# GEGLU feed-forward on one core: x's second half on ScalarE's queue, and six first products ahead of any second

## The chip, the cores and the metric

The kernel runs on one core of one Trainium2 chip. A core has five engines, each with its own instruction stream: TensorE (PE in the profile; its weight loads are PEld), VectorE (DVE), ScalarE (ACT), GpSimd (POOL) and SyncE (SP). Transfers from the chip's main memory run on 16 DMA engines that all of them share. SyncE and ScalarE can put a transfer on a queue of their own (q1 is SyncE's, q10 ScalarE's). The metric is the time of one execution on the device, in microseconds. The kernel before took 277.13 us (median of three runs, 276.82 to 277.15).

## The reference

```python
B, S, D, F = 32, 32, 1024, 3584
def reference(x, w_gate, w_up, w_down):      # x: (B, S, D), all bfloat16
    return (gelu_tanh(x @ w_gate) * (x @ w_up)) @ w_down
```

There are 1024 rows of x, so three products of 1024 x 1024 x 3584 have to be done.

## The kernel before, in words

The kernel has two stages. Stage 1 computes g = gelu(x w_gate) * (x w_up), transposed, into the tile `gT` (28 blocks of 128 columns of F, each 128 x 1024). Stage 2 multiplies g by w_down. Both replace eight half-size products of a 2 x 2 block scheme by seven, with sums of blocks formed on VectorE and GpSimd. Only the start of stage 1 is touched by the change.

**Names.** `B11`, `B21` are the two D halves of the first 512 rows of x, transposed (tile `xt0`); `B12`, `B22` are the D halves of the last 512 rows (tile `xt1`). x lies row by row in memory, so these are loaded with a transposing transfer (`dma_start_transpose`). `WG[c]` holds 256 columns of w_gate, which is two blocks of 128. Its D half `0:KH` (KH = 4 slices of 128) feeds a block's first product, its half `KH:DT` the second. `WU[c]` holds 512 columns of w_up.

**Blocks.** `first_products(i)` (lines 199 to 207) sends four matmuls of B11 with the first half of block i into a PSUM tile A[i], and ScalarE then copies A[i] to `E1`. `second_products(i)` (209 to 214) adds four matmuls with B21 to the same A[i], and ScalarE puts the gelu of it into `GL`. The second product of a block may begin only when ScalarE has copied A[i]. `seed(i)` (218) copies E1 into a PSUM tile X[i], which later products are added to. T1 to T4 are four sums of B11, B12, B21, B22, made on VectorE (`t_sum`, 158 to 161, called at 269 to 272), and they feed the products that come behind (`y` at 286, `x` in `sixth_products`, `seventh_products`, `fourth_product`).

**Order.** `tc.manual_schedule()` means that each engine runs its instructions in the order in which the code writes them. At the start TensorE multiplies a tile of zeros NWARM = 11 times (line 139). SyncE issues, in this order: B11 (131), B21 (144), the second half of gate tile 1 (145), gate tiles 2 and 3 (146, 147), half of w_up tile 0 (148), gate tile 4 (149), xt1 (150), gate tile 5 (151), the rest of w_up tile 0 (152). ScalarE issues three loads: the first half of gate tile 0 at the start (132), the first half of gate tile 1 behind the third multiplication of zeros, and the second half of gate tile 0 behind the eleventh (143). The first ten blocks are then worked in the groups (0 to 3), (4, 5), (6, 7), (8, 9): the first products of a group, then its second products (274 to 280).

The names `A` and `y` live in four PSUM tiles of tag `q`, the zeros' results and `X` in four of tag `p`.

Of the kernel before, what the change touches and what calls it, by code (L numbers as in the profile page):

```python
# [12 lines left out]
def kernel(  # L13
# [18 lines left out]
    nc = tc.nc  # L32
    P = nc.NUM_PARTITIONS
# [4 lines left out]
    xf = x.flatten_outer_dims()  # L38
    of = out.flatten_outer_dims()
    N, D = xf.shape  # L40
    F = w_gate.shape[1]
    NB = 512
    DT = D // P
    KH = DT // 2
# [2 lines left out]
    DB = 512  # L47
    NDB = D // DB
    assert N == 2 * NB and DT % 2 == 0 and D % DB == 0 and FT % 4 == 0
    NWARM = 11  # L50
    LEAD = 10
    ALONE = (4, 7, 10, 13, 16, 19, 22, 25)
    KF = FT // 2
# [22 lines left out]
    B11, B21 = xt0[:, :KH, :], xt0[:, KH:, :]  # L76
# [6 lines left out]
    def load_gate(c, queue, lo=0, hi=DT):  # L83
        if c not in WG:
            WG[c] = gw.tile([P, DT, 2 * P], bf16, name="gw", tag="gw")
        queue.dma_start(
            out=WG[c][:, lo:hi, :], in_=wg_r[:, lo:hi, 2 * c * P : (2 * c + 2) * P]
        )

    def load_up(c, lo=0, hi=4):  # L90
        if c not in WU:
            WU[c] = uw.tile([P, DT, 4 * P], bf16, name="uw", tag="uw")
        nc.sync.dma_start(
            out=WU[c][:, :, lo * P : hi * P],
            in_=wu_r[:, :, (4 * c + lo) * P : (4 * c + hi) * P],
        )
# [4 lines left out]
    def a11(i):  # L101
        return block(WG, 2, i, 0)

    def a12(i):
        return block(WG, 2, i, 1)
# [4 lines left out]
    def a22(i):  # L110
        return block(WU, 4, i, 1)
# [12 lines left out]
    def psum_p(name):  # L124
        return psum.tile([P, NB], fp32, name=name, tag="p")

    def psum_q(name):
        return psum.tile([P, NB], fp32, name=name, tag="q")

    with tc.manual_schedule():  # L130
        nc.sync.dma_start_transpose(out=B11, in_=xf[0:NB, 0 : KH * P])  # L131
        load_gate(0, nc.scalar, 0, KH)
        zt = opool.tile([P, NB], bf16, name="zt", tag="o")
        nc.vector.memset(zt, 0.0)
        warm = [psum_p("warm") for _ in range(4)]
# [2 lines left out]

        for n in range(NWARM):
            nc.tensor.matmul(warm[n % 4], lhsT=zt[:, 0:P], rhs=zt, start=True, stop=True)  # L140
            if n in (2, NWARM - 1):
                nc.scalar.activation(table, warm[n % 4][:, 0:8], ACT.Copy)
                load_gate(int(n == 2), nc.scalar, *((0, KH) if n == 2 else (KH, DT)))
        nc.sync.dma_start_transpose(out=B21, in_=xf[0:NB, KH * P : D])
        load_gate(1, nc.sync, KH, DT)
        load_gate(2, nc.sync)
        load_gate(3, nc.sync)
        load_up(0, 0, 2)
        load_gate(4, nc.sync)
        nc.sync.dma_start_transpose(out=xt1, in_=xf[NB:N, :])  # L150
        load_gate(5, nc.sync)
# [6 lines left out]
        def t_sum(name, a, b, step=2):  # L158
            for k in range(0, KH, step):
                ks = slice(k, k + step)  # L160
                nc.vector.tensor_tensor(T[name][:, ks, :], a[:, ks, :], b[:, ks, :], ALU.subtract)
# [19 lines left out]
        def copy_a22(i):  # L181
            nc.scalar.activation(C22[i], a22(i), ACT.Copy)

        A, E1, GL = {}, {}, {}

        def pair_product(ps, lhs, rhs, first, cuts):
            for lo, hi in zip(cuts, cuts[1:]):
                for p, l in zip(ps, lhs):
                    for k in range(lo, hi):
                        nc.tensor.matmul(  # L190
                            p,
                            lhsT=l[:, k, :],
                            rhs=rhs[:, k, :],
                            start=(first and k == 0),
                            stop=(k == KH - 1),
                            skip_group_check=True,
                        )

        def first_products(*blocks, cuts=(0, KH)):
            for i in blocks:  # L200
                A[i] = psum_q("a")
            pair_product([A[i] for i in blocks], [a11(i) for i in blocks], B11, True, cuts)
            for i in blocks:
                if i % 2 == 0:
                    pool, tag = (xpool, "e1") if i == LEAD - 2 else (ring, "ring")
                    E1[i // 2] = pool.tile([P, 2, NB], fp32, name="e1", tag=tag)
                nc.scalar.activation(E1[i // 2][:, i % 2, :], A[i], ACT.Copy)  # L207

        def second_products(*blocks, cuts=(0, KH)):
            pair_product([A[i] for i in blocks], [a12(i) for i in blocks], B21, False, cuts)  # L210
            for i in blocks:
                if i % 2 == 0:
                    GL[i // 2] = half.tile([P, 2, NB], bf16, name="gl0", tag="half")
                nc.scalar.activation(GL[i // 2][:, i % 2, :], A[i], ACT.Gelu_apprx_tanh)  # L214
# [3 lines left out]
        def seed(i):  # L218
            X[i] = psum_p("x")
            nc.scalar.activation(X[i], E1[i // 2][:, i % 2, :], ACT.Copy)  # L220
# [3 lines left out]
        def ahead():  # L224
            nonlocal done
            if done < FT:
                first_products(done)
            second_products(done - 1)
            done += 1
# [40 lines left out]
        t_sum("T2", B22, T["T1"])  # L270
        t_sum("T3", B22, B12)
        t_sum("T4", B21, T["T2"])
        between = {4: lambda: seed(0), 6: lambda: seed(1), 8: lambda: copy_a22(0)}
        for blocks in ((0, 1, 2, 3), (4, 5), (6, 7), (8, 9)):
            for n in blocks:
                first_products(n)
            if blocks[0] in between:
                between[blocks[0]]()
            for n in blocks:
                second_products(n)  # L280
        for k in range(KH):
            nc.scalar.activation(T["B22"][:, k, :], B22[:, k, :], ACT.Copy)
        copy_a22(1)
        for i in range(2):
            Y[i] = psum_q("y")
        pair_product(
            [Y[0], Y[1]], [S1[0], S1[1]], T["T1"], True, range(KH + 1)
        )
        first_products(LEAD)
        sixth_products(0, 1)  # L290
        first_products(LEAD + 1)
# [88 lines left out]
        B21 = lambda j: V21[j]  # L380
# [149 lines left out]
```

## Time and profile before

| what | from | value |
|---|---|---|
| median of three runs | the times | 277.13 us |
| profiled execution, time on the device | the times | 276.81 us |
| its span in the trace | the page | 275.0 us |
| TensorE busy | the page, part 1 | 269.7 us, 98% of the span |
| DMA engines, bytes moved | the page, part 3 | 26.42 MB, 96 GB/s over the span |
| first matmul of block 0 starts | the timeline | 6.14 us |
| first matmul of a second product starts | the timeline | 10.57 us |
| first product with T1 starts | the timeline | 24.19 us |
| last matmul of stage 1 and 2 | the timeline | about 271.5 us |

The span is counted from the first instruction that the trace holds; the execution's own time has some 1.8 us more around it. A matmul's duration in the rows (about 380 ns) is that of one passing through a filled pipeline; from start to start it is 0.216 us for the 128 x 512 shape in bfloat16, as 48 of them from 10.57 to 20.92 us show. "Landing" is the time from the issue of a transfer to its completion as seen by who waits for it.

### The profile page before, as it was taken

How to read it: one execution, taken by the hardware profiler on the slowest of the kernel's cores; microseconds unless marked ns; L12 is line 12 of the kernel's file. 1: busy time of each engine (PE TensorE's matmuls, PEld its weight loads, DVE VectorE, ACT ScalarE, POOL GpSimd, SP SyncE). 2: the span in 40 equal slices, each digit the busy share in tenths (PEclk: the TensorE clock that was granted, in tenths of full speed). 3: DMA queues.
4: the chain of work that ended last, by engine and by line, in shares of the span. 5: the costliest groups of instructions: out<-in, count | busy, mean ns of one | idle time of the engine just before them, and what ended most of it. 6: DMA issues, size and time to landing. Idle time of an engine off the chain costs nothing.

```text
span 275.0 us, 3348 instructions
## 1 busy us (share of the span) xinstructions
PE 269.7 (98%) x1187; PEld 189.9 (69%) x1187; DVE 189.1 (69%) x227; ACT 138.1 (50%) x238; POOL 87.1 (32%) x81
## 2 busy tenths in 40 slices
PE   8999999999999999999999999999999999999994
PEld 2345677768777687776877768764447888888883
DVE  0059875766667666676666766759994999999900
ACT  2578655656656666566665666531100072860311
POOL 0000073854558545585455854600000000000000
PEclk9999999999999999999999999999999999999999
DMA  8999402062400024216260202359602000000321
GB/s 170 279 288 254 155 1 76 25 206 80 150 2 0 0 87 145 76 31 199 87 220 0 76 2 77 117 181 328 216 0 76 2 0 0 1 2 0 116 76 38
DMA packets 40960, 26.42 MB, mean 96 GB/s; under 512 B 9200, under 2 KB 40944, under 8 KB 40944
## 3 DMA queue, kind: packets, MB, share of 16 engines
q1 hardware_dynamic: 39216, 25.30, 31.6%
q10 hardware_dynamic: 1728, 0.92, 1.3%
q8 instruction: 9, 0.15, 0.2%
q14 instruction: 7, 0.06, 0.1%
HBM read 22.02 MB, written 2.10 MB: 88 GB/s over the span
## 4 chain that ended last, share of the span: by engine, by line
PE 95%; DMA 3%; SPq 1%; ACT 0%; issue 0%
PE x L190 19%; PE x L385 18%; PE y L115 18%; PE a L190 16%; PE x L115 9%; PE y L385 9%; PE z L385 4%; DMA xt<-in_x_dram 3%; PE y L190 1%; SPq L131 1%; ACT o_sb L497 0%
## 5 line engine op out<-in xcount | busy, mean ns | idle before, releaser
L190 PE MATMUL x<-T,s 128*128 128x512 f32 x224 | 63.4, 407 | 0.0
L190 PEld LDWEIGHTS x<-T,s 128*128 128x128 f32 x224 | 41.8, 188 | 10.7
L190 PE MATMUL a<-xt,gw 128*128 128x512 bf16 x192 | 45.0, 382 | 0.6 <-DMA xt<-in_x_dram 0.5
L253 DVE TENSOR_TENSOR u<-y,e 128x512 bf16<-128x512 f32 x28 | 19.3, 692 | 33.0 <-ACT e L251 32.2
L179 POOL TENSOR_TENSOR s<-gw,s 128x512 fp32r<-128x512 bf16 x22 | 26.0, 1180 | 48.4 <-PE y L115 47.7
L190 PEld LDWEIGHTS <-gw 128*128 128x128 bf16 x192 | 17.5, 98 | 24.7 <-issue 5.7
L175 DVE TENSOR_TENSOR s<-s,gw 128x512 fp32r<-128x512 f32 x24 | 34.5, 1437 | 0.0
L260 ACT ACTIVATE gl<-h 128x512 bf16<-128x512 bf16 x28 | 17.7, 631 | 28.1 <-DVE h L258 28.1
L240 DVE TENSOR_TENSOR gT<-gl,x 128x512 bf16<-128x512 bf16 x28 | 19.2, 687 | 17.6 <-PE x L115 17.6
L115 PE MATMUL x<-T,c 128*128 128x512 f32 x112 | 30.3, 393 | 0.0
L115 PE MATMUL y<-B,s 128*128 128x512 f32 x112 | 30.2, 391 | 0.0
L170 POOL TENSOR_TENSOR s<-uw 128x512 fp32r<-128x512 bf16 x25 | 29.1, 1162 | 0.0
L115 PE MATMUL y<-T,s 128*128 128x512 f32 x104 | 27.8, 389 | 0.0
L385 PE MATMUL x<-tc,sc 128*128 128x512 f32 x112 | 25.7, 389 | 0.0
L207 ACT ACTIVATE e<-a 128x512 f32<-128x512 f32 x28 | 16.7, 597 | 16.5 <-PE a L190 16.5
L251 ACT ACTIVATE e<-x 128x512 f32<-128x512 f32 x28 | 16.7, 599 | 16.1 <-PE x L190 16.1
L171 POOL TENSOR_TENSOR s<-gw,uw 128x512 fp32r<-128x512 bf16 x21 | 24.4, 1161 | 0.0
L115 PEld LDWEIGHTS y<-B,s 128*128 128x128 f32 x112 | 21.0, 188 | 4.7
L115 PEld LDWEIGHTS x<-T,c 128*128 128x128 f32 x112 | 20.9, 188 | 4.8 <-ACT e L251 0.5
L385 PEld LDWEIGHTS x<-tc,sc 128*128 128x128 f32 x112 | 21.0, 188 | 4.4
L115 PEld LDWEIGHTS y<-T,s 128*128 128x128 f32 x104 | 19.5, 188 | 4.1
L214 ACT ACTIVATE gl<-a 128x512 bf16<-128x512 f32 x28 | 16.7, 596 | 6.8 <-PE a L190 6.5
(57 smaller groups left out, 342.0 us busy)
## 6 DMA issues: line engine op xcount, KB each, us to landing
uw<-in_w_up_dram SPq DMA_DIRECT2D x6, 1024.0 KB, 6.4
gw<-in_w_gate_dram SPq DMA_DIRECT2D x10, 512.0 KB, 4.0
v<-in_w_down_dram SPq DMA_DIRECT2D x5, 512.0 KB, 3.4
v<-in_w_down_dram SPq DMA_DIRECT2D x4, 640.0 KB, 7.9
v<-in_w_down_dram SPq DMA_DIRECT2D x8, 256.0 KB, 4.4
out_dram<-o_sb SPq DMA_DIRECT2D x15, 128.0 KB, 1.7
uw<-in_w_up_dram SPq DMA_DIRECT2D x2, 512.0 KB, 6.7
gT<-in_w_gate_dram SPq DMA_DIRECT2D x2, 512.0 KB, 6.1
```

The source lines that it names most:

```text
L115: nc.tensor.matmul(ps, lhsT=lhs[:, k, :], rhs=rhs[:, k, :], start=(first and k == 0), stop=(k == KH - 1), skip_group_check=True,)
L170: engine.tensor_tensor(S1[i], a21(i), a22(i), ALU.add)
L171: engine.tensor_tensor(S3[i], a11(i), a21(i), ALU.subtract)
L175: nc.vector.tensor_tensor(S2[i], S1[i], a11(i), ALU.subtract)
L179: engine.tensor_tensor(S4[i], a12(i), S2[i], ALU.subtract)
L190: nc.tensor.matmul(p, lhsT=l[:, k, :], rhs=rhs[:, k, :], start=(first and k == 0), stop=(k == KH - 1), skip_group_check=True,)
L207: nc.scalar.activation(E1[i // 2][:, i % 2, :], A[i], ACT.Copy)
L214: nc.scalar.activation(GL[i // 2][:, i % 2, :], A[i], ACT.Gelu_apprx_tanh)
L240: nc.vector.tensor_tensor(gT[:, i, 0:NB], GL[i // 2][:, i % 2, :], X[i], ALU.mult)
L253: nc.vector.tensor_tensor(U1[i], Y[i], e3, ALU.add)
L260: nc.scalar.activation(G1[i], h1, ACT.Gelu_apprx_tanh)
L385: nc.tensor.matmul(ps, lhsT=lhs[:, i, t * P : (t + 1) * P], rhs=rhs[:, i, :], start=(first and j == 0 and i == 0), stop=(last and j == JF ...
```

## The change

Three things are edited, all within the first 25 us.

1. **Loads.** B21 goes from SyncE's queue (second there) to ScalarE's, behind the third multiplication of zeros. ScalarE keeps one other load, a quarter of gate tile 0 (two of its eight slices). Everything else that ScalarE loaded is now on SyncE's queue, directly behind B11: the next quarter of gate tile 0, the first halves of gate tiles 1 and 2, the second half of tile 0, the second halves of tiles 1 and 2, the first half of tile 3, half of w_up tile 0 (so this lies between the halves of gate tile 3), the second half of gate tile 3, gate tile 4, and from there as before. In the built program, ScalarE's transpose waits for the completion of the transpose of B11, and SyncE's load of gate tile 4 waits for the completion of the transpose of B21.
2. **Order of products.** The first products of blocks 0 to 5 all come before any second product. Blocks 0 and 1 share their first products in two cuts: slices 0 and 1 of both blocks, then slices 2 and 3. A[4] and A[5] take PSUM tiles of tag `p`. `seed(0)` moves from behind block 5's first product to behind block 4's second product.
3. **Zeros.** NWARM is 10 in place of 11, and the second small activation on the zeros' result is gone.

The number of matmuls on x and the weights, the bytes loaded, the sums and the evictions are the same.

```diff
-    NWARM = 11
+    NWARM = 10
...
         nc.sync.dma_start_transpose(out=B11, in_=xf[0:NB, 0 : KH * P])
-        load_gate(0, nc.scalar, 0, KH)
+        load_gate(0, nc.scalar, 0, 2)
...
         for n in range(NWARM):
             nc.tensor.matmul(warm[n % 4], lhsT=zt[:, 0:P], rhs=zt, start=True, stop=True)
-            if n in (2, NWARM - 1):
+            if n == 2:
                 nc.scalar.activation(table, warm[n % 4][:, 0:8], ACT.Copy)
-                load_gate(int(n == 2), nc.scalar, *((0, KH) if n == 2 else (KH, DT)))
-        nc.sync.dma_start_transpose(out=B21, in_=xf[0:NB, KH * P : D])
+                nc.scalar.dma_start_transpose(out=B21, in_=xf[0:NB, KH * P : D])
+        for piece in ((0, 2, KH), (1, 0, KH), (2, 0, KH), (0, KH, DT)):
+            load_gate(piece[0], nc.sync, *piece[1:])
         load_gate(1, nc.sync, KH, DT)
-        load_gate(2, nc.sync)
-        load_gate(3, nc.sync)
+        load_gate(2, nc.sync, KH, DT)
+        load_gate(3, nc.sync, 0, KH)
         load_up(0, 0, 2)
+        load_gate(3, nc.sync, KH, DT)
         load_gate(4, nc.sync)
...
             for i in blocks:
-                A[i] = psum_q("a")
+                A[i] = psum_p("a") if i in (4, 5) else psum_q("a")
...
-        between = {4: lambda: seed(0), 6: lambda: seed(1), 8: lambda: copy_a22(0)}
-        for blocks in ((0, 1, 2, 3), (4, 5), (6, 7), (8, 9)):
-            for n in blocks:
-                first_products(n)
-            if blocks[0] in between:
-                between[blocks[0]]()
-            for n in blocks:
-                second_products(n)
+        between = {6: lambda: seed(1), 8: lambda: copy_a22(0)}
+        first_products(0, 1, cuts=(0, 2, KH))
+        for n in range(2, 6):
+            first_products(n)
+        for n in range(6):
+            second_products(n)
+            if n == 4:
+                seed(0)
+        for n in (6, 8):
+            first_products(n)
+            first_products(n + 1)
+            between[n]()
+            second_products(n)
+            second_products(n + 1)
```

## The prediction

> **What bounds the kernel now.** I read the page first, then the chain that ended last in its first 48 us, then the timeline of the first 25 us, then the DMA queues in stretches of 0.2 to 1 us.
>
> ```profile
> PE 269.7 (98%) x1187; PEld 189.9 (69%) x1187; DVE 189.1 (69%) x227; ACT 138.1 (50%) x238; POOL 87.1 (32%) x81
> PE 95%; DMA 3%; SPq 1%; ACT 0%; issue 0%
> ```
>
> TensorE is the bound from end to end. Only 4% of the chain is not TensorE, and it lies at the start:
>
> ```profile
> 0.74 1.42 SPq L131
> ...
> 2.21 8.22 DMA xt<-in_x_dram
> 10.43 0.14 issue
> 10.57 13.97 PE a L190 x64
> 24.54 1.84 PE y L190 x8
> ```
>
> The chain is B11's issue, then B21's transfer (landed at 10.43), then TensorE without a break. Whatever the change wins or loses must be won or lost by where TensorE stands behind B21. The timeline shows how it gets there:
>
> ```profile
> 2.21 4.95 SPq L144 DMA_TRANSPOSE xt<-in_x_dram  x1
> ...
> 6.14 3.91 PE L190 MATMUL a<-xt,gw 128*128 128x512 bf16 x16
> ...
> 10.57 10.52 PE L190 MATMUL a<-xt,gw 128*128 128x512 bf16 x48 [0.52 <-DMA xt<-in_x_dram]
> ```
>
> The landing row of `xt` gives 5.4 us as the shortest: 0.74 + 5.4 = 6.14, so B11's landing is what starts block 0. The matmuls of zeros start 0.427 us apart, the first real ones at 6.14, 6.51 and 6.86, and from there 0.216 us apart (48 in 10.35 us). So the array turns to double speed at about 6.78. Sixteen first products are through at 6.86 + 14 x 0.216 = 9.88; B21's matmuls start at 10.57. TensorE stands 0.69 us for B21, and there is no other wait of it on the page behind that.
>
> Last the DMA queues, q1 SyncE's and q10 ScalarE's, in the stretches 4 to 5, 7 to 8 and 8.6 to 8.8 us (packets, MB, share):
>
> ```profile
> q1 hardware_dynamic: 1122, 0.29, 127.1%
> ```
>
> ```profile
> q1 hardware_dynamic: 1010, 0.26, 114.1%
> ```
>
> ```profile
> q10 hardware_dynamic: 124, 0.06, 113.7%
> q1 hardware_dynamic: 8, 0.00, 4.5%
> ```
>
> Packets of 256 bytes are a transpose, of 512 bytes a gate load. From 4 to 5 only B11 flows, though ScalarE's load of gate tile 1 had been issued at 2.77; it flows from 5.2, when B11 is through. From 7 to 8 only B21 flows, though ScalarE's second half of gate tile 0 had been issued at 6.18; it flows from 8.4 to 9.4, and meanwhile SyncE's queue stands. Two transfers on two queues thus took turns, whole transfer by whole transfer, at 0.29 MB/us. B21's last data went at 8.6, but its 16 completions only at 9.2 to 9.6, behind ScalarE's load, and it landed at 10.43.
>
> **The change, part by part.**
>
> *B11 lands earlier.* B11 flowed from 2.7 to 5.45 beside ScalarE's 0.26 MB. Half of that load moves behind B11: 0.13 MB / 0.29 = 0.45 us. B11 lands at 6.14 - 0.45 = 5.69. Bounds: 0 (6.14, if something else held it) and 0.94 (5.20, if it flows without its pause at 3.6 to 4.0 and nothing in its way). I take 0.45, the bytes.
>
> *One multiplication of zeros fewer.* Ten end at 1.19 + 10 x 0.427 = 5.46, before B11 lands, so it costs nothing as long as B11 lands behind 5.46; it would have cost 0.2 (eleven end at 5.89). TensorE starts at 5.69. To 6.78 it does 1.09 / 0.427 = 2.55 matmuls, to 6.86 another 0.37: 2.9, where it had done 2.0 before. Gain 0.9 x 0.216 = 0.20 us. [...]
>
> *Six first products.* 24 matmuls in place of 16 stand before the first need of B21: they end at 6.86 + 21.1 x 0.216 = 11.41. Before, the same amount of work would have stood at 10.57 + 8 x 0.216 = 12.30. So the most that can be won is 0.89 us, and with L for B21's landing (0.14 from landing to matmul, as before) the gain is 12.30 - max(11.41, L + 0.14): full up to L = 11.27, nothing at L = 12.16, a loss behind it.
>
> *B21 on ScalarE's queue.* ScalarE waits for B11's completion (5.69, start 0.05 behind), then issues. From its issue to its landing, the nearest row is B11 itself: 5.4 us, a transpose of the same size on an empty queue with the other queue's loads beside it. L = 5.74 + 5.4 = 11.14. Lower bound 10.1 (the same less the 0.45 of foreign bytes, and B11 landed 0.5 earlier); upper bound: B21's whole 8.22 from issue to landing, 13.96. I take 5.4: like B11's, the queue is empty and nothing of its own kind is ahead, which is not so for the 8.22 (B11 lay ahead of it). So no stall.
>
> *The gate pieces.* Nothing is added in bytes. Behind B11 (through at 5.0) SyncE's queue gives the quarter of tile 0 by 5.45, tile 1 by 6.35, tile 2 by 7.25, tile 0's second half by 8.15 or, if B21's 1.8 us come between, 10.0; each lands 0.8 later. TensorE needs them at 7.1, 7.9, 9.7 and 11.41. All in time; a pause of half a microsecond behind B11, as the load behind xt1 has at 21.3 to 21.8, would cost 0.2. SyncE's seven or eight issues of 0.37 to 0.58 each run ahead of the flow. Its load of gate tile 4 now waits for B21 (11.14, 10.82 before); 3.7 MB are queued before it, which at the pace of before (2.29 MB by 11, then 0.29 per us) last to 15.8. xt1 flows when it did, and lands at 21.8 as before.
>
> *ScalarE.* Blocked to 5.69, then one issue: 1.42 us as SyncE's on an empty queue. Free at 7.2; A[0] is done at 7.5. Each eviction takes 0.60 against 0.86 of matmuls: hidden. The dropped activation and two issues cost nothing. The upper bound is SyncE's 4.95: rival 3.
>
> *T1 to T4.* TensorE arrives 0.89 earlier, xt1 does not. VectorE has the last quarter of T1 at 24.36, needed before at 24.19 + 3 x 0.46 = 25.57; T2's second half 26.63, needed 27.83; T4's 31.18, needed 32.83. The least slack is 1.2 us, so 0.3 is left. If xt1 slips by more than 0.3, the rest is lost again; cost 0 taken, bound 0.5.
>
> *Sum.* 0.20 + 0.69 = 0.89 us. Against the profiled execution 276.81 - 0.89 = 275.92; that one lies 0.32 under the median, so 277.13 - 0.89 = **276.2 us**. From 25 us on TensorE does the same work in the same order.
>
> **The rivals.**
>
> *1, slower: B21 is starved on ScalarE's queue.* Nowhere in the trace does a transpose on one queue meet a full queue of gate loads on the other. If engines alternate there by small portions, a 256-byte packet for each 512-byte one, B21 gets a third of 0.29 MB/us: 0.524 / 0.097 = 5.4 us from about 7.7 (B11's first packet came 1.96 behind its issue), landed 0.75 behind that: 13.85. Then 13.99 - 12.30 = 1.7 lost, **278.8 us**. It decides from a landing of 12.16. Against it: gate tile 0's second half ran its 1.0 us through while q1 had B21's completions waiting. For it: where one queue stood, it may just not have been filled yet. [...]
>
> *2, no change: turns are whole transfers, but B21 has to give way more than once.* Before its start, in its pause (B11 and B21 both show one, at 3.6 and 6.8) or ahead of its completions, a SyncE load of 0.26 MB takes 0.9 us. One such turn more than in B11's case: L = 12.04, gain 0.1, **277.0 us**; two: 277.9. For it: B21's completions waited exactly so in the trace. Against it: B11's did not.
>
> *3, slower: ScalarE's issue takes 4.95 us.* Free at 10.7, it has 14 operations of 0.65 to do before block 6's E1 is out: 19.8, while TensorE wants it at 11.41 + 32 x 0.216 = 18.3. 1.5 lost of 0.89 won, **277.7 us**. It decides from ScalarE free at 9.2. Against it: ScalarE's issues took 0.37 while SyncE hung in its 4.95, so that one was its own queue's.
>
> **How the numbers follow.** About 0.2% (0.55 us) is what a measurement of this kernel can tell from no change. The forecast, or a gain over 0.55 with a landing up to 11.6: 0.45. Rival 2 and other landings from 11.6 to 12.7: same, 0.24. Rival 1 and two turns or more: 0.24; rival 3, or xt1 late by over 1.5: 0.07; together slower 0.31. The likeliest case alone holds 276.0 to 276.6 (B11 between 5.2 and 5.9). The range goes from 275.9 to 278.8, rival 1's end, which leaves out some 0.05 below and 0.1 above.
>
> **What would show it.** Block 0 starts at 5.6 to 5.8. `xt`'s transpose on ScalarE is issued at about 5.75 in 1.4 us and lands near 11.1; no idle time of TensorE before the second products, which begin at 11.4; the first product with T1 starts at 23.3 (24.19 before), with no wait of TensorE for VectorE behind it. Wrong would be: 256-byte packets of q10 thinly spread beside 512-byte ones of q1 from 7.7 to 13 (rival 1), one block of q1 packets inside B21's (rival 2), a ScalarE issue over 3 us (rival 3), or a gap before `y` at 23.3 (xt1 late).

## The result, and the profile after

The changed kernel takes 283.35 us (median of five, 282.80 to 284.13) against 277.13 for the kernel before (276.82 to 277.27). The ratio is 1.0231, interval 1.0219 to 1.0242: slower by 6.2 us, where 0.9 us faster was forecast, and outside the range of 275.9 to 278.8. The profiled execution took 283.01 us, its span is 281.2 us.

The engines' shares of the chain that ended last, on the page of the changed kernel, and its first pieces in order of time (start, us, what):

```profile
PE 93%; DMA 6%; issue 0%; ACT 0%
```

```profile
0.74 4.34 DMA xt<-in_x_dram
5.08 0.02 issue
5.10 11.74 DMA xt<-in_x_dram
16.84 0.14 issue
16.97 5.08 PE a L192 x15
22.05 0.05 issue
22.10 8.80 PE a L192 x40
```

B11 lands at 5.08 (6.14 before). Then the chain is one transfer of 11.74 us: B21, issued at 5.10, lands at 16.84 (10.43 before). The timeline shows the stop that it makes, and the two issues that run beside each other:

```profile
2.22 4.65 SPq L86 DMA_DIRECT2D gw<-in_w_gate_dram  x7
...
5.10 4.34 ACTq L143 DMA_TRANSPOSE xt<-in_x_dram  x1
...
5.43 6.00 PE L192 MATMUL a<-xt,gw 128*128 128x512 bf16 x24
...
16.97 10.47 PE L192 MATMUL a<-xt,gw 128*128 128x512 bf16 x39 [5.54 <-DMA xt<-in_x_dram]
```

The 24 first products start at 5.43 and are done when the forecast had it, and then TensorE stands for 5.5 us. Two lines of q10 and q1 from 11.2 to 11.6 us (packets, MB, share of the 16 engines), and two from 15.2 to 15.6:

```profile
q10 hardware_dynamic: 176, 0.05, 76.9%
q1 hardware_dynamic: 77, 0.04, 52.3%
```

```profile
q1 hardware_dynamic: 227, 0.11, 118.0%
q10 hardware_dynamic: 15, 0.00, 2.6%
```

In the first stretch B21's 256-byte packets and SyncE's 512-byte packets go side by side, some two to one, 0.08 MB in 0.4 us where one queue alone moves 0.12. The packets themselves took longer: the share times 16 engines times 0.4 us, divided by the count, is 28 ns for one of B21's and 43 ns for one of SyncE's, where B11 alone shows 18 ns (the prediction's stretch from 4 to 5) and SyncE alone 33 ns (the second stretch). B21's data begin at 8.3 and end at 13.5. By 13.6 q10 has shown 2048 packets behind its first load, which at 256 bytes are B21's 0.52 MB. In the second stretch its 15 packets take 11 ns each. They are among 32 that trickle out behind the data, between 14.0 and 16.3, while SyncE's loads flow at full rate (0.11 MB in these 0.4 us). I take these 32 for B21's completions, since it lands 0.5 us behind the last; the trace does not name them.

The last part of the loss is in the table of stretches (length, busy time of PE, PEld, DVE, ACT, POOL, then the granted TensorE clock, DMA share, GB/s):

```profile
13.00:14.00 1.00, 0.00 (x0) 0.00 (x0) 0.00 (x0) 0.00 (x0) 0.00 (x0) 0.79 1.20 237
14.00:15.00 1.00, 0.00 (x0) 0.00 (x0) 0.00 (x0) 0.00 (x0) 0.00 (x0) 0.50 1.21 285
...
19.00:20.00 1.00, 1.00 (x4) 0.38 (x3) 0.96 (x3) 0.47 (x1) 0.00 (x0) 0.50 1.08 317
20.00:21.00 1.00, 1.00 (x5) 0.39 (x4) 1.00 (x3) 0.43 (x1) 0.00 (x0) 0.80 1.25 271
```

The clock is halved at about 13.6, some 2.2 us after TensorE's last matmul, and comes back at 20.4, 3.4 us after it resumed. The eight matmuls in between start 0.43 us apart, twice the 0.216 of the others.

The account: the second products start at 16.97 where the same amount of work would have stood at 12.30 before, 4.67 us. The first product with T1 starts at 30.55 against 24.19, 6.36 us; the difference of 1.7 is the half clock. Behind that the two kernels run nearly alike (6.20 us between the profiled executions).

### The profile page after: what moved, and what is told of

Its sections match the earlier page's. It is cut to its first block, busy times and chain, and to the rows that moved or that the text cites. A ratio compares the mean times of both kernels' runs of the same rounds, so it can differ in the third digit from the quotient of the medians.

```text
span 281.2 us, 3332 instructions
## 1 busy us (share of the span) xinstructions
PE 270.5 (96%) x1172; PEld 190.3 (68%) x1186; DVE 188.9 (67%) x227; ACT 137.4 (49%) x237; POOL 87.1 (31%) x81
## 4 chain that ended last, share of the span: by engine, by line
PE 93%; DMA 6%; issue 0%; ACT 0%
PE x L192 18%; PE x L393 18%; PE y L115 17%; PE a L192 16%; PE y L393 9%; PE x L115 9%; DMA xt<-in_x_dram 6%; PE z L393 4%; PE y L192 1%; ACT o_sb L505 0%
## 5 line engine op out<-in xcount | busy, mean ns | idle before, releaser
L192 PE MATMUL a<-xt,gw 128*128 128x512 bf16 x182 | 46.4, 395 | 6.1 <-DMA xt<-in_x_dram 5.5
L242 DVE TENSOR_TENSOR gT<-gl,x 128x512 bf16<-128x512 bf16 x28 | 19.2, 686 | 17.9 <-PE x L115 17.9
L216 ACT ACTIVATE gl<-a 128x512 bf16<-128x512 f32 x28 | 16.7, 596 | 13.2 <-PE a L192 13.0
```

What stands on the lines that cost most here:

```text
L192: nc.tensor.matmul(p, lhsT=l[:, k, :], rhs=rhs[:, k, :], start=(first and k == 0), stop=(k == KH - 1), skip_group_check=True,)
L242: nc.vector.tensor_tensor(gT[:, i, 0:NB], GL[i // 2][:, i % 2, :], X[i], ALU.mult)
```

## The experiments

The kernel before was timed beside each set of runs: 276.74, 276.88 and 276.98 us.

**B21 back on SyncE's queue.** In the changed kernel, the transpose of B21 goes directly behind B11:

```diff
+        nc.sync.dma_start_transpose(out=B21, in_=xf[0:NB, KH * P : D])
         for piece in ((0, 2, KH), (1, 0, KH), (2, 0, KH), (0, KH, DT)):
             load_gate(piece[0], nc.sync, *piece[1:])
```

> The changed kernel with one move undone: B21 goes back to SyncE's queue, directly behind B11; the order of products, the pieces of the gate tiles and the ten zeros stay. If the queue of B21 is the cause (theory Q), B21 flows from 4.5 to 6.6 us and lands by 8, the quarter of gate tile 0 behind it lands at about 7.9 and holds up block 0's third matmul of each block by 0.7 us, and the second products start at about 12.2 without a wait: 277.0 us, within 0.5. If the new order of products or the PSUM tiles of A[4] and A[5] carry the loss (rival O), it stays over 282.

Measured: 277.02 us, ratio 1.0018 (0.9999 to 1.0038). The new order of products, the PSUM tiles and the cut gate tiles cost nothing that can be seen; moving one line back removes the loss. The quarter of gate tile 0 held TensorE up as expected (0.58 us, at 7.54).

**B21 fifth on SyncE's queue.** As before, but behind the first half of gate tile 2:

```diff
         for piece in ((0, 2, KH), (1, 0, KH), (2, 0, KH)):
             load_gate(piece[0], nc.sync, *piece[1:])
+        nc.sync.dma_start_transpose(out=B21, in_=xf[0:NB, KH * P : D])
+        load_gate(0, nc.sync, KH, DT)
```

> As the changed kernel, with B21 on SyncE's queue behind the first half of gate tile 2, so that only what the six first products need is ahead of it. Theory Q: B21 flows whole from about 7.3 to 9.3 and lands near 10.2, gate tile 0's second half lands near 11, TensorE goes from its first product at 5.4 on without a stop and starts the second products at 11.3 to 11.5: 276.1 us, faster than before by 0.8 to 1.1. Rival O: over 282.

Measured: 276.26 us, ratio 0.9981 (0.9971 to 0.9991), and once more:

> The run with B21 fifth on SyncE's queue once more, in five rounds: 276.0 to 276.4, 0.1 to 0.3% faster than before.

Measured: 275.90 us, ratio 0.9964 (0.9951 to 0.9976). This version beats the kernel before by 0.5 us in the first set of runs and by 1.1 in the second. The timeline of the first shows 64 matmuls, the 24 first products and all behind them up to block 8, in one row:

```profile
5.41 14.27 PE L193 MATMUL a<-xt,gw 128*128 128x512 bf16 x64
```

There is no long stop: TensorE waits briefly at 10.8 for the second half of gate tile 0 (the weight load at 10.87 stood 0.61 us for it), and again near 23 for T1. B21 landed 5.3 us after its issue at 3.96. So the gain that the sum promised was to be had, and the changed kernel lost it to the queue. How much of it is owed to the six first products is not shown: B21 landed at 9.26 here, about when sixteen first products that start at 5.41 would be through (8.87 at 0.216 us each, some tenths later with the first ones at 0.43, an estimate from the rows), and no run has this order of loads with the old order of products.

**The queue alone, on the kernel before.** B21 goes to ScalarE's queue behind the first half of gate tile 1, all else as before:

```diff
+                if n == 2:
+                    nc.scalar.dma_start_transpose(out=B21, in_=xf[0:NB, KH * P : D])
...
-        nc.sync.dma_start_transpose(out=B21, in_=xf[0:NB, KH * P : D])
```

> The kernel before with one move alone: B21 issued on ScalarE's queue behind the first half of gate tile 1; order of products, pieces and zeros as before. If the queue carries the whole loss (theory Q), B21 waits for B11 (6.1), is mixed with SyncE's 2.9 MB of loads and lands at 16 to 18, TensorE waits from 9.9 and comes back at half clock: 6 to 7.5 us for the wait and 1.7 for the clock, 284 to 286.5; the six first products of the changed kernel then recover some 1.7 of what the queue costs. If the move is harmful only with the gate pieces cut as in the changed kernel, under 280.

Measured: 286.21 us, ratio 1.0339 (1.0317 to 1.0361). The move alone costs 9.2 us, 3 more than the whole change. Its timeline:

```profile
5.32 2.27 SPq L93 DMA_DIRECT2D uw<-in_w_up_dram  x1
6.01 5.13 ACTq L145 DMA_TRANSPOSE xt<-in_x_dram  x1
...
11.26 0.51 ACTq L86 DMA_DIRECT2D gw<-in_w_gate_dram  x1
...
17.58 12.23 PE L191 MATMUL a<-xt,gw 128*128 128x512 bf16 x48 [7.94 <-DMA gw<-in_w_gate_dram]
```

B21, issued at 6.01, shows its first packets at 10.5, right behind the 1.3 MB of gate tiles that SyncE had issued before it. To 12.0 it flows almost alone, then mixed with the w_up load (0.33 MB/us for both from 12.0 to 13.2), and its completions come mostly at 15.2 to 15.6, behind SyncE's loads. It lands at 16.4; ScalarE's next load, held up behind the long issue, lands at 17.54 and is what TensorE waits for at last, so some 1.1 of the 9.2 us are that load's.

**SyncE held while B21 flows.** B21 stays on ScalarE's queue, but behind the second half of gate tile 0 SyncE gets a transpose of one slice of xt1, which waits for B21's completion, so that nothing is queued beside most of it:

```diff
             load_gate(piece[0], nc.sync, *piece[1:])
+        nc.sync.dma_start_transpose(out=xt1[:, 0:1, :], in_=xf[NB:N, 0:P])
         load_gate(1, nc.sync, KH, DT)
...
-        nc.sync.dma_start_transpose(out=xt1, in_=xf[NB:N, :])
+        nc.sync.dma_start_transpose(out=xt1[:, 1:, :], in_=xf[NB:N, P:])
```

> As the changed kernel, B21 still on ScalarE's queue, but SyncE issues only what the first products and block 0's second product need (up to the second half of gate tile 0), and then a transpose of one slice of xt1, which waits for B21's completion. So no SyncE load is queued beside most of B21. If SyncE's full queue starves B21 (theory Q, sharing), B21 flows from about 8.3 at 0.29 MB/us, is through by 10.5 and lands by 11.5; the loads behind it come late, so 277 to 279. If a transpose is slow because ScalarE issues it (rival S: its issue took 4.3 us and its first packet came 3.2 us behind it), B21 lands at 14 or later and the time is 281 or more.

Measured: 278.83 us, ratio 1.0070 (1.0050 to 1.0089). B21's piece of the chain, and its queue from 9.2 to 9.6 us:

```profile
5.22 5.04 DMA xt<-in_x_dram
```

```profile
q10 hardware_dynamic: 456, 0.12, 128.2%
```

It lands at 10.26, as fast as the forecast had it (5.04 against 5.4 us), though ScalarE issued it, and though that issue took 3.14 us. So the transpose on ScalarE was not slow in itself; with SyncE's loads beside it, in the changed kernel, it took 11.74. (What this kernel loses, 2 us against the kernel before, comes from the held loads: TensorE waits 2.44 us for a gate half, and then runs at half clock from its restart at 14.76 to 17.9, some 1.6 us more. Part of both is made up by the earlier first products.)

**SyncE held two loads later.** The holding transpose stands behind the second halves of gate tiles 1 and 2, so 0.52 MB are queued beside B21:

> As the run with SyncE held, but the holding transpose stands two loads later (behind the second halves of gate tiles 1 and 2), so that 0.52 MB are queued beside B21 where there were none (landing at 10.26) and 1.5 MB in the changed kernel (landing at 16.84). If B21's completion comes only when SyncE's backlog is through (theory Q), it lands at 11.8 to 13: B21's 0.52 and the 0.52 at 0.2 to 0.29 MB/us from 8.0. If what hurts is the number of packets in flight only while B21's data flow, the landing is at 11 to 11.5.

Measured: 282.04 us (a single run; before 276.88). B21's piece of the chain:

```profile
5.66 9.22 DMA xt<-in_x_dram
```

It lands at 14.88, behind either expectation. From 9.2 to 12.8 both queues together move 0.19 MB/us. SyncE's last packet goes between 14.0 and 14.4, B21's last completions too. So the landing falls together with the end of what SyncE had queued; in the changed kernel the last completion comes at 16.3, when SyncE's flow begins to thin out (it ends at 17.5). The rate is worse than I had reckoned, and from 13.2 to 14.4, with little left on either queue, the rest trickled at 0.035 MB/us. Sharing alone does not explain that; it stays open. The four runs with B21 on ScalarE's queue, by packets in stretches of 0.1 to 0.4 us:

| kernel | issued | first data | last data | landed |
|---|---|---|---|---|
| held behind tile 0 | 5.22 | 7.6 | 9.9 | 10.26 |
| held two loads later | 5.66 | 8.7 | 13.5 | 14.88 |
| the changed kernel | 5.10 | 8.3 | 13.5 | 16.84 |
| before, move alone | 6.01 | 10.5 | 13.6 | 16.4 |

**The half clock.** 26 multiplications of zeros between the first and the second products of the changed kernel keep TensorE busy:

```diff
+        for n in range(26):
+            nc.tensor.matmul(warm[2 + n % 2], lhsT=zt[:, 0:P], rhs=zt, start=True, stop=True)
         for n in range(6):
             second_products(n)
```

> The changed kernel with 26 multiplications of zeros between the first and the second products, 26 x 0.216 = 5.6 us, which is the wait for B21. If 1.7 of the 6.2 us lost are the half clock that the trace shows from 13.8 to 20.3 us (theory C), the granted clock stays 1.0 and the time is 281.3 to 281.9. If the half clock costs nothing, 283.3 or more, since the zeros can only be in the way.

Measured: 281.96 us, ratio 1.0192 (1.0175 to 1.0209). In the table of stretches its clock stays whole:

```profile
14.00:15.00 1.00, 1.00 (x7) 0.47 (x5) 0.00 (x0) 0.00 (x0) 0.00 (x0) 1.00 1.20 289
```

B21 landed at 17.15 here, 0.3 later than in the changed kernel; with that added back to the 1.3 us between the two profiled executions (281.70, 283.01), the half clock is worth 1.6 us.

**The queues exchanged.** B11 and B21 on SyncE, six gate pieces on ScalarE:

```diff
             if n == 2:
                 nc.scalar.activation(table, warm[n % 4][:, 0:8], ACT.Copy)
-                nc.scalar.dma_start_transpose(out=B21, in_=xf[0:NB, KH * P : D])
+                for piece in ((0, 2, KH), (1, 0, KH), (2, 0, KH), (0, KH, DT), (1, KH, DT), (2, KH, DT)):
+                    load_gate(piece[0], nc.scalar, *piece[1:])
...
+        nc.sync.dma_start_transpose(out=B21, in_=xf[0:NB, KH * P : D])
```

> The queues exchanged: B11 and B21 both from SyncE, one behind the other, and six gate pieces (the second quarter of tile 0 to the second half of tile 2) from ScalarE behind its second small activation, so that a full queue of 512-byte packets stands on the other side of the transpose. If a full queue on the other side is what starves a transpose, whichever engine issues it (theory Q), B21's packets are mixed with ScalarE's and it lands well behind the 7 us that it took in the run with B21 second on SyncE: at 10 to 13, 277 to 279 us. If the transfers are served in the order in which they were issued (rival F, issue order: B21 at 2.21, the first piece at about 2.95), B21 flows whole from 4.4 to 6.6, lands by 8, and the late quarter of tile 0 holds up the start as there: 277.0.

Measured: 276.35 us, ratio 0.9989 (0.9978 to 1.0000). B21, issued at 2.21 in 3.98 us, was mixed with ScalarE's pieces from 6.4 to 8.5, and its completions, 31 packets at 10.0 to 10.8, let it land at 11.6, 9.4 us after its issue. So theory Q held for the landing, by the late completions: here B21 was on SyncE's queue and landed 3.1 us behind its last data, with ScalarE's loads flowing at 0.29 MB/us from 8.8 to 10.4. The flow itself was not starved: B21's data were over by 8.5, since the two queues together moved 0.3 MB/us here, not 0.2. Its price of the time was wrong, and rival F gave neither the landing nor the time: the landing was just soon enough for TensorE.

**One gate half back on ScalarE, and nine zeros.** The version with B21 fifth on SyncE, with the second half of gate tile 0 issued by ScalarE behind the last zeros, and the same with NWARM = 9:

```diff
+            if n == NWARM - 1:
+                nc.scalar.activation(table, warm[n % 4][:, 0:8], ACT.Copy)
+                load_gate(0, nc.scalar, KH, DT)
...
-        load_gate(0, nc.sync, KH, DT)
```

> As the run with B21 fifth on SyncE's queue (276.26), with the second half of gate tile 0 back on ScalarE, behind the last zeros (issued at about 5.6), as the kernel before has it. That run lost 0.6 us of DMA flow between 8.8 and 9.6, behind B21, and TensorE had to wait for that half at 10.87 and for T1 at 23. One load waiting on the other queue should fill the gap as in the kernel before: the half lands at 10.0 to 10.4, xt1 by 21.6, no wait at T1: 275.7 to 276.0, against 276.26. If two queues are a loss in any case, it is 276.3 or more.

> As the run before with nine zeros: TensorE is free at 5.03 and B11 lands at 5.08 to 5.25, so the first products start 0.2 to 0.35 us earlier, at half clock: 0.1 to 0.15 us less than with ten zeros, 275.6 to 275.9. If the zeros matter for the clock (its doubling comes later by their number), the same or 0.1 more.

Measured: 276.83 us, ratio 1.0008 (0.9994 to 1.0022), and 276.94 us, ratio 1.0007 (0.9994 to 1.0021). Both expectations failed. B21's piece of the chain with ten zeros:

```profile
4.00 8.25 DMA xt<-in_x_dram
```

One load of 0.26 MB on the other queue, issued at 5.04, took B21 from 5.3 to 8.25 us: the two trickle side by side from 8.0 to 10.4 at 0.18 MB/us, and TensorE stood 2.08 us for B21 (1.47 in the run with nine zeros, where B21 took 7.66). The first products began at 5.05 with nine zeros and at 4.97 with ten, since the zeros of that run happened to be over at 4.93, and no difference of the times is left.

**The same half, earlier, in the kernel before.**

```diff
-            if n in (2, NWARM - 1):
+            if n in (2, 3):
```

> The kernel before, with ScalarE's load of the second half of gate tile 0 issued behind the fourth zeros in place of the eleventh: at about 3.2 us, before B21 begins to flow, in place of 6.18, when B21 was flowing. The run with that half on ScalarE and B21 fifth on SyncE mixed the two (B21 landed at 12.25), the kernel before did not (10.43). If what is issued before the transpose flows is mixed with it, B21 lands at 11 to 12.5 and the time is 277.4 to 279. If the two take turns because ScalarE's queue holds little, the half flows behind gate tile 1's, B21 behind it, landing 10.4 to 11, 276.7 to 277.4.

Measured: 276.44 us, ratio 0.9984 (0.9974 to 0.9993): faster than before by some 0.5 us, which neither case had foreseen. The two did not mix. The chain:

```profile
2.21 7.58 DMA xt<-in_x_dram
9.79 0.14 issue
9.93 13.97 PE a L190 x64
```

ScalarE's half now flows before B21, not between B21's data and its completions, so B21's landing comes at 9.79 in place of 10.43. Half a microsecond of the 0.89 forecast was thus within reach with the old order of products.

## Why the prediction was wrong, point by point

- **What bounds the kernel** held: TensorE, and the time is set by where it stands behind B21.
- **B11 lands earlier** held in kind: 5.08, under the 5.20 that was its lower bound, 5.69 taken. The same start of the program gave 5.20, 5.43 and 5.64 in the first held run, the one with 26 zeros and the second held run, so much of it is the execution's.
- **One multiplication of zeros fewer** was to cost nothing if B11 landed behind 5.46. It landed before, and TensorE was in its zeros until 5.43. This did not matter beside the rest, and nine zeros brought no time that could be measured. The moment of double speed differed from one execution to the next: the rows of ten zeros are 4.45 us long here, 4.39 in the first run with B21 fifth, 3.84 in the run with SyncE held and 3.74 in the one with a gate half back on ScalarE.
- **Six first products** held: they were through by 11.4, as worked out, and the formula 12.30 - (L + 0.14) gives -4.68 for the landing at 16.84, which is the measured start.
- **The gate pieces and T1 to T4** held in effect: the first products ran from 5.43 without a stop. That xt1 would flow when it did before did not hold, since it stands behind a load that waits for B21: T1's first sum starts at 24.62, 21.86 before. TensorE came later still, and `y` at 30.55 shows no wait.
- **B21 on ScalarE's queue** is the step that failed: 5.4 us from issue to landing taken, 11.74 measured, beyond even the upper bound of a landing at 13.96. The 6.3 us more are, against B11's own passage: 1.2 until the first data (3.2 us after the issue, 1.96 for B11), when q1 alone shows packets, 1.1 MB from 4.4 to 8.3, about the five loads (1.2 MB) that SyncE had begun to issue by 4.71; 2.5 in the data (5.2 us from first to last against 2.7), which were mixed with gate loads (176 packets to 77 in the stretch above); 2.6 in the completions (3.3 us behind the data against 0.7). The row of B11 was a bad neighbour: beside B11 the other queue held 0.5 MB, beside B21 it had packets in every stretch of 0.4 us.
- **The completions** were in front of me in the profile before: 0.6 to 1.0 us behind B21's data, behind ScalarE's load. I priced this as a single turn of 0.9 us in rival 2; in the changed kernel it was 3.3 us from the last data to the landing.
- **The clock** behind a stop was missing from the sum and from all rivals. I had the half-speed start of the array in the rows (0.427 us from one matmul to the next, with the granted clock shown as 1.00), and did not ask what a long stop would do. It is 1.6 to 1.7 us of the 6.2.
- **Rival 1** (0.24 with its kin) named the mechanism that came: small packets of q10 between those of q1. Its 5.4 us for the data came out (5.2), but by luck: it had reckoned one packet for one at 0.29 MB/us, and the packets went some two to one at 0.17 MB/us for both queues (8.8 to 12.8). Its landing of 13.85 lacked 0.6 until the first data (8.3 against 7.7) and 2.6 in the completions, and its 278.8 the clock too. **Rival 3** was half right: ScalarE's issue took 4.34 us, against my argument that its own queue alone decides, but the evictions were not what TensorE waited for.

## What to carry to other kernels

Where two queues feed the same DMA engines, a transfer that the next step waits for should be on the queue whose order already puts it there. Here, in the changed kernel, one transpose moved back to the one queue, behind the gate halves needed sooner, left it 0.5 to 1.1 us faster than the kernel before; on the other queue it cost 6 us (9 with the old order of products). In these runs the second queue was no fast lane: B21 on it showed its first data 2.4 to 4.5 us after its issue, was mixed with SyncE's loads in three of the four runs of the table, and in these landed 1.4 to 3.3 us behind its last data. A price for a transfer should be taken from a row in which the other queue is as full as it will be. And a stop of TensorE is not priced by its length alone: behind the four stops of 2.44 to 7.94 us here it came back at half clock, for another 3.2 to 5.3 us.

## What the runs showed of the hardware that was not expected

- A transpose (256-byte packets) mixed with plain loads (512-byte packets) of another queue moved 0.17 to 0.19 MB/us in all in three runs (the changed kernel from 8.8 to 12.8, SyncE held two loads later from 9.2 to 12.8, and ten zeros with one gate half back on ScalarE from 8.0 to 10.4), against 0.29 for either alone. In the run with the queues exchanged, and in part of the one with the move alone, the mixture moved 0.30 and 0.33, and the packets of the latter took no longer than alone (18 ns and 27 ns from 12.4 to 12.8). Which side has the transpose does not decide it, since both kinds occur with it on either; what does stays open.
- Why the kernel before, and the run with ScalarE's half issued at 3.26, showed clean turns, and the one with that half at 5.04 beside B21's issue (4.00 to 7.18) did not, was not settled either. That the two issues ran at the same time goes with mixing in the changed kernel and with its absence in the first held run (SyncE's issues ended at 4.78, ScalarE's began at 5.22), but in the kernel before a load issued at 6.18, within B21's 2.21 to 7.16, did not mix.
- Late completions went with work on the other queue in the runs above. From the last data to the landing it was 3.3 us in the changed kernel, with SyncE's loads flowing beside it, and 0.4 in the run where SyncE was held. What holds a completion back was not shown.
- The clock was halved 2.0 to 2.2 us after TensorE's last matmul in the changed kernel and in both held runs, but 4.6 us after it in the run with the move alone. A stop of 2.44 us was enough in the first held run, and a stop of 2.08 us left the clock whole in the run with ten zeros and a gate half on ScalarE. So no one delay fits these runs. What agrees between them is the length of the half clock. The stretches in which it begins and ends, first with SyncE held two loads later, then with the move alone:

```profile
13.00:14.00 1.00, 0.00 (x0) 0.00 (x0) 0.00 (x0) 0.00 (x0) 0.00 (x0) 0.76 0.26 49
20.00:21.00 1.00, 1.00 (x5) 0.44 (x4) 0.00 (x0) 0.60 (x1) 0.00 (x0) 0.82 1.12 288
```

```profile
14.00:15.00 1.00, 0.00 (x0) 0.00 (x0) 0.17 (x1) 0.00 (x0) 0.00 (x0) 0.61 1.18 319
21.00:22.00 1.00, 1.00 (x6) 0.50 (x5) 0.00 (x0) 0.60 (x1) 0.00 (x0) 0.98 0.97 213
```

A mean of 0.76 over 1 us means half clock for 0.48 of it, so it lasted from 13.52 to 20.36 and from 14.22 to 21.04. With 13.58 to 20.40 in the changed kernel and 14.52 to 17.94 in the first held run, the half clock lasted 6.84, 6.82, 6.82 and 3.42 us: once or twice the same 3.4 us. How much of that falls on work depends on where the stop lies in it: 3.2 us in the first held run, 3.4 in the changed kernel, 3.5 with the move alone, 5.3 with SyncE held two loads later.
